# Order of masking, checks and subtractions in a fused top-k attention and feed-forward kernel

## Chip, core and metric

The kernel runs on one core of a Trainium2 chip. The metric is the device time of one execution in microseconds (us). A core has five engines that each take instructions in order from their own queue and meet through semaphores: TensorE (PE), VectorE (DVE), ScalarE (ACT), GpSimd (POOL) and SyncE (SP, which here only issues DMA transfers).

## What is computed

Batch 8, 8 heads, 576 positions, head size 64; then a feed-forward block of 4608 rows, width 512, hidden width 2048. Everything is float32.

```python
scores = scale * np.matmul(q, k.transpose(0, 1, 3, 2))
kth = np.partition(scores, -32, axis=-1)[..., -32:-31]
scores = np.where(scores >= kth, scores, -1e9)
scores = scores - np.max(scores, axis=-1, keepdims=True)
attn = np.exp(scores)
attn = attn / (np.sum(attn, axis=-1, keepdims=True) + 1e-09)
x = np.matmul(attn, v)          # then (B,H,S,D) -> (B*S, H*D)
h = x @ w_in
g = h - np.tanh(h)
out = g @ w_out
```

Of each row of 576 scores only the 32 largest keep a weight. The row's threshold is its 32nd largest score.

## The kernel before

The attention is cut into 144 steps. A step is one pair of heads and 128 query rows (or the last 64 rows of two pairs), so it holds two rows of 576 scores per partition, t = 0 and 1. The main loop in `run` runs over n and works on several steps at once, each at another stage:

- `scores(n + 1)`: PE multiplies q and k into PSUM (scps, L237), ACT copies them to SBUF (sc, L245). There is one PSUM buffer for this.
- `search(n)`: DVE finds the 32 largest of each row. It first takes the smaller and the larger of the two halves of a row (L267, L268, into one of two buffers ab), then the eight largest of the smaller halves (L270), then four rounds of the eight largest (L275) and their removal (L278). Between rounds it calls `between`, which brings in other DVE work.
- `mask(n - 1)`: POOL works out the threshold tb (L294, two small instructions) and the shift nb (L303). For t = 0 and 1 ACT writes a penalty into z (L307), zero for scores at or above the threshold, and POOL subtracts it from the score (L310). Then POOL writes the two checks `bad` (L314): whether the largest 32 of the search could have missed one among the smaller halves. The checks read ab, so the search after next, which takes the same buffer, waits for them at L267. If any check ever fails, the program runs a second time with an exact search; the profiled execution does not.
- `expo(n - 1)`: ACT takes the exponential with row sums (L330), POOL adds the epsilon (rd, L340). `invert` (DVE) and `spread` (POOL, rx, L355) prepare the division.
- Turning the weights, so that keys lie on partitions: in the 18 steps of batch 0 (`pe=True`) PE transposes z in 128 x 128 blocks (zt, L409) and ACT copies them into et (L412): two copies of 512 columns at the beginning of a step, one of 128 later. In all other steps DVE transposes 32 x 32 blocks (L376) and DMAs rearrange them (L390, on SP's queue).
- `values`: PE multiplies by v (av, L433) and turns rx (L441); ACT copies (xs, L445); POOL multiplies (xT, L457, or xTr, L448).

When all pairs of heads of a block of rows (a unit, 128 or 256 rows) are done, its feed-forward work is put on a list as small items, and `deal` spends them between the stages at a rate that a planner works out (`rate`). `ffn_h` multiplies by w_in (hps, L486); each time 512 columns are full, ACT takes tanh (th, L498) and copies h (g, L499), and POOL subtracts (g, L500). `ffn_o` multiplies g by w_out in eight parts of two blocks (ops, L507); part p reads the subtractions in the order in which they were made. ACT copies the result (ot, L517) and SP stores it. th, ot and a temporary f of the weight conversion share four buffers.

The weights are converted on the chip during steps 0 to 10 of batch 0, 32 pieces in all, two to four a step, called from `between` (`convert`): per piece DVE (L157, L163), ACT (f L158, L161, and L166), DVE (L169) and POOL (L172), before the piece's buffer takes the next load.

All of this is written out in one program order; no scheduler moves anything. In one turn of the loop the order is: `spread` and `values` of older steps; then, in batch 0, the transposes with the two large et copies; then `mask(n - 1)`; then `search(n)`; then feed-forward items, `scores(n + 1)`, the small et copy, `expo(n - 1)`, and more feed-forward items. An engine's queue has its instructions in exactly this order, so on ACT the two et copies stand ahead of the penalties, and on POOL a g subtraction of one turn stands ahead of the next turn's tb.

Of the kernel before, what the change touches and what calls it, by code (L numbers as in the profile page):

```python
# [8 lines left out]
AF = mybir.ActivationFunctionType  # L9
ALU = mybir.AluOpType  # L10
FP32 = mybir.dt.float32
# [5 lines left out]
BIG = 2.0**80  # L17
# [31 lines left out]
def kernel(  # L49
# [9 lines left out]
    nc = tc.nc  # L59
    P = nc.NUM_PARTITIONS  # L60
    B, H, S, D = q.shape
# [15 lines left out]
    scale = 1.0 / float(D) ** 0.5  # L77
# [5 lines left out]
    def pool(name, bufs, **kw):  # L83
        return ctx.enter_context(tc.tile_pool(name=name, bufs=bufs, **kw))
# [7 lines left out]
    zpool = pool("z", 2)  # L92
# [191 lines left out]
    def mask(n, exact):  # L284

        x = st[n]
        sc, m = x["sc"], x.pop("m")
        scf = sc[:].rearrange("p t s k -> p t (s k)")
        tb = mpool.tile([P, 2], FP32, tag="tb", name="tb")
        if exact:  # L290
            nc.gpsimd.tensor_scalar(tb[:], m[:, :, TOP - 1], BIG, None, ALU.mult)
        else:
            for t in range(2):
                nc.gpsimd.tensor_scalar(  # L294
                    tb[:, t : t + 1],
                    m[:, t, TOP - 1 : TOP],
                    m[:, t, TOP - 9 : TOP - 8],
                    BIG,
                    ALU.min,
                    ALU.mult,  # L300
                )
        nb = mpool.tile([P, 2], FP32, tag="nb", name="nb")
        nc.gpsimd.tensor_scalar(nb[:], m[:, :, 0], -scale, None, ALU.mult)  # L303
        z = zpool.tile([P, 2 * S], FP32, tag="z", name="z")
        zv = z[:].rearrange("p (t k) -> p t k", t=2)
        for t in range(2):
            nc.scalar.activation(  # L307
                zv[:, t, :], scf[:, t, :], AF.Relu, bias=tb[:, t : t + 1], scale=-BIG
            )
            nc.gpsimd.tensor_tensor(zv[:, t, :], scf[:, t, :], zv[:, t, :], ALU.subtract)  # L310
        if not exact:
            ab = x.pop("ab")
            for t in range(2):
                nc.gpsimd.tensor_scalar(  # L314
                    bad[:, t, n : n + 1],
                    ab[:, t, S2 + 7 : S2 + 8],
                    BIG,
                    tb[:, t : t + 1],
                    ALU.mult,
                    ALU.is_gt,  # L320
                )
        x.update(z=z, zv=zv, nb=nb)

    rds = {}
# [24 lines left out]
    def spread(n):  # L349

        if steps[n].last:
            rd = rds.pop(n)
            nq = steps[n].nq
            rx = rxs[n] = xpool.tile([P, 2, 2, D], FP32, tag="rx", name="rx")
            nc.gpsimd.tensor_copy(  # L355
                rx[:, 0:nq], rd[:, 0:nq].unsqueeze(3).to_broadcast([P, nq, 2, D])
            )
# [36 lines left out]
    def turn_pe(n):  # L394

        g, z = steps[n], st.pop(n)["z"]
        if g.rem:
            et = et_rem
        elif g.i:
            et = ets.pop(n - 1)  # L400
        else:
            et = etpool.tile([P, 4 * S], FP32, tag="et", name="et")[:]
        ets[n] = et
        et = tiles(et, g.nq)[:, :, :, g.i, :].rearrange("p a k j -> p k a j")
        for k0 in range(0, KC, J):
            kn = min(J, KC - k0)
            zt = zt_ps.tile([P, 512], FP32, tag="zt", name="zt")
            for k in range(kn):
                nc.tensor.transpose(  # L409
                    zt[:, k * P : (k + 1) * P], z[:, (k0 + k) * P : (k0 + k + 1) * P], ident[:]  # L410
                )
            nc.scalar.copy(  # L412
                et[:, k0 : k0 + kn],
                zt[:, 0 : kn * P].rearrange("p (k a j) -> p k a j", a=NG, j=G),
            )
            if k0:
                yield
# [53 lines left out]
            u.xT = p.tile([P, CD, N], FP32, tag=u.tag, name=u.tag)  # L471
        return u.xT

    cur = {}

    def ffn_h(u, item):

        w = u.n
        per = 2 * P // w
        for f in range(item * per, (item + 1) * per):  # L480
            j, fo = f // FJ, (f % FJ) * P
            s = f * w % 512
            if s == 0:
                cur[u] = h_ps.tile([P, 512], FP32, tag="h", name="hps")
            for c in range(CD):
                nc.tensor.matmul(  # L486
                    cur[u][:, s : s + w],
                    w_in[j][:, c, fo : fo + P],
                    u.xT[:, c, 0:w],
                    start=(c == 0),  # L490
                    stop=(c == CD - 1),
                )
        if item % 2:
            th = thpool.tile([P, 512], FP32, tag="th", name="th")
            if item % 4 == 1:
                u.g.append(gpool.tile([P, 2, 512], FP32, tag="g", name="g"))
            g = u.g[-1][:, item % 4 // 2, :]
            nc.scalar.activation(th[:], cur[u][:], AF.Tanh)  # L498
            nc.scalar.copy(g, cur[u][:])  # L499
            nc.gpsimd.tensor_tensor(g, g, th[:], ALU.subtract)  # L500

    def ffn_o(u, i, part):
        if part == 0:
            cur[u] = h_ps.tile([P, DM], FP32, tag="h", name="ops")
        for f in range(2 * part, 2 * part + 2):
            o = f * u.n + i * P
            nc.tensor.matmul(  # L507
                cur[u][:],
                u.g[o // 1024][:, o % 1024 // 512, o % 512 : o % 512 + P],
                w_out[f // FJ][:, f % FJ, :],  # L510
                start=(f == 0),
                stop=(f == CF - 1),
            )
        if part < CF // 2 - 1:
            return
        ot = thpool.tile([P, DM], FP32, tag="th", name="ot")
        nc.scalar.copy(ot[:], cur[u][:])  # L517
        for rows, dst in u.blocks[i]:
            nc.sync.dma_start(dst, ot[rows, :])
# [50 lines left out]
    def run(exact):  # L570
# [9 lines left out]
        for i, (b, hp) in enumerate(pairs):  # L580
            n = next(n for n, g in enumerate(steps) if (g.b, g.hp) == (b, hp))
# [56 lines left out]
        def here(i):  # L638
            return 0 <= n + i < NS

        def between(i):
            for fn in at_round.pop((n, i), []):
                fn()
            if i == 0 and here(-2):
                invert(n - 2)
                if not steps[n - 2].pe:
                    turn_z(n - 2)
# [9 lines left out]
        for u in begun:  # L657
            k = 2 if u.tag == "xT" else 1
# [5 lines left out]
        def rate():  # L664


            have, low, high = len(work), 0.0, None
            coming = sorted((t, u.n // 8) for u, t in ready.items() if t > n)
            for t, k in coming + [(NS + 4, 0)]:
                r = have / max(t - n, 1)  # L670
                high = r if high is None else min(high, r)
                have += k
            for u, t in begun.items():
                if t > n and u in before:
                    need = [i + 1 for i, x in enumerate(work) if x[1] is before[u]]
                    if need:
                        low = max(low, need[-1] / (t - n))
            return max(low, high)
# [11 lines left out]
        for n in range(-4, NS + 4):  # L690
            pe = here(-2) and steps[n - 2].pe
            if here(-3) and not steps[n - 3].pe:
                spread(n - 3)
            for m in (n - 4, n - 3):
                if 0 <= m < NS and steps[m].last and steps[m].lag == n - m:
                    values(m)
            share, usable = rate(), converted[0]
            if pe:
                w = turn_pe(n - 2)
                next(w)  # L700
            if here(-1):
                mask(n - 1, exact)
            if here(0):
                search(n, exact, between)
            elif here(-2):
                between(0)
            if here(-2) and not pe and steps[n - 2].last:
                spread_keys(n - 2)
            if pe:
                spread(n - 2)  # L710
            deal(0.4)
            if here(1):
                scores(n + 1)
            if pe:
                next(w)
            if here(-1):
                expo(n - 1)
            deal(0.2)
            if pe and steps[n - 2].last:
                values(n - 2)  # L720
            deal(0.2)
            for fn in todo.pop(n, []):
                fn()
            deal(0.2)
# [4 lines left out]
    with tc.manual_schedule():  # L729
        run(False)  # L730
# [10 lines left out]
    with tc.If(again > 0):  # L741
        with tc.manual_schedule():
            run(True)
# [29 lines left out]
```

## Time and profile before

| what | us |
|---|---|
| four runs, median | 1548.53 |
| four runs, lowest and highest | 1547.87, 1550.42 |
| the profiled execution | 1551.0 |
| its span, first to last instruction | 1549.2 |
| PE busy | 1440.7 (93%) |
| DVE busy | 1347.7 (87%) |
| POOL busy | 941.3 (61%) |
| ACT busy | 883.0 (57%) |
| chain that ended last: PE's share | 73% |
| chain that ended last: DVE's share | 10% |

Busy times are sums over the span; register, semaphore and DMA-issuing instructions are not counted. The chain that ended last is followed back from the last instruction, at each step to what released it. A line of the timeline names the start and the time of an instruction, its engine, its line in the kernel, what it writes and reads, and in brackets how long its engine had stood idle before it and which engine's work ended that. In the lists of waits a line says which engine's instruction waited for which other, and for how long in total, how many times, and the longest.

The instructions that the change moves, with the count and mean time of one:

| line | engine, what | count | mean ns |
|---|---|---|---|
| L294 | POOL, threshold tb | 288 | 299 |
| L303 | POOL, shift nb | 144 | 254 |
| L307 | ACT, penalty z | 288 | 769 |
| L310 | POOL, z subtraction | 288 | 1411 |
| L314 | POOL, check bad | 288 | 323 |
| L412 | ACT, et copy of 512 columns | 36 | 591 to 605 |
| L500 | POOL, g subtraction | 144 | 1276 |

### The profile page before, as it was taken

To read this page: it belongs to the slowest core of one execution; us is meant where nothing else is said; L and a number is where in the kernel's file an instruction comes from. 1 tells how busy PE (TensorE), PEld (TensorE's weight loads), DVE (VectorE), ACT (ScalarE), POOL (GpSimd) and SP (SyncE) were. 2 spreads that over 40 slices of the span, in tenths; PEclk is the share of its full clock that TensorE was granted. 3 is DMA by queue.
4 is the path that set the end of the run, shared out by engine and by line. 5 is a ranking of instruction groups with operands and counts; after the bars stand their busy time and mean duration, and the time that the engine had idled before them with its cause. 6 is when DMAs were issued, how large, how long until landed. Compare 5 with 4: busy or idle time off the path is not lost.

```text
span 1549.2 us, 25298 instructions
## 1 busy us (share of the span) xinstructions
PE 1440.7 (93%) x7428; PEld 912.2 (59%) x7428; DVE 1347.7 (87%) x3828; ACT 883.0 (57%) x1567; POOL 941.3 (61%) x1525
## 2 busy tenths in 40 slices
PE   2556899899999999999999999999999999999997
PEld 1345467455565665656566665656566665656673
DVE  7987889999999999999999999999999999997300
ACT  4886767556565565656565565656565565655320
POOL 3777667667565675757565675757565675746420
PEclk9777899999999999999999999999999999999999
DMA  9944113324443354234433354234443345322200
GB/s 255 359 160 159 50 28 67 89 69 94 104 92 76 83 105 103 70 78 97 103 88 79 80 107 102 70 79 97 100 90 80 80 98 110 81 64 59 73 10 16
DMA packets 258835, 147.42 MB, mean 95 GB/s; under 512 B 210048, under 2 KB 217216, under 8 KB 258688
## 3 DMA queue, kind: packets, MB, share of 16 engines
q1 hardware_dynamic: 256912, 145.49, 38.3%
q8 instruction: 62, 1.02, 0.3%
q14 instruction: 85, 0.70, 0.1%
q10 hardware_dynamic: 1776, 0.22, 0.1%
HBM read 61.85 MB, written 9.44 MB: 46 GB/s over the span
## 4 chain that ended last, share of the span: by engine, by line
PE 73%; DVE 10%; SPq 5%; ACT 4%; issue 3%; DMA 3%; POOL 2%; DVEq 0%; ACTq 0%; POOLq 0%
PE ops L507 27%; PE hps L486 26%; PE av L433 9%; PE scps L237 8%; SPq L390 4%; DVE ab L278 3%; DVE m L275 3%; PE av L441 2%; SPq L200 1%; DMA zx<-in_moe_w_in_dram 1%; ACT z L307 1%; PE zt L409 1%; DVE spare L376 1%; DVE ab L270 1%; DVE ab L267 1%
## 5 line engine op out<-in xcount | busy, mean ns | idle before, releaser
L507 PE MATMUL ops<-w_out,g 128*128 128x512 f32 x1152 | 525.4, 602 | 0.0
L486 PE MATMUL hps<-xT,w_in 128*128 128x256 f32 (+1 forms) x2176 | 473.7, 373 | 1.2 <-POOL xT L457 1.2
L275 DVE MAX8 m<-ab 128x8 f32<-128x288 f32 (+1 forms) x1152 | 464.3, 444 | 0.0
L310 POOL TENSOR_TENSOR z<-sc,z 128x576 f32<-128x576 f32 x288 | 400.2, 1411 | 83.8 <-ACT z L307 83.8
L486 PEld LDWEIGHTS hps<-xT,w_in 128*128 128x128 f32 x2176 | 392.5, 193 | 73.4 <-issue 16.0
L278 DVE MATCH_REPLACE8 ab<-m,ab 128x288 f32<-128x288 f32 x864 | 376.1, 443 | 0.0
L507 PEld LDWEIGHTS ops<-w_out,g 128*128 128x128 f32 x1152 | 212.0, 192 | 243.6 <-issue 240.0
L307 ACT ACTIVATE z<-sc,tb 128x576 f32<-128x576 f32 x288 | 207.6, 769 | 153.8 <-POOL tb L294 153.8
L500 POOL TENSOR_TENSOR g<-g,th 128x512 f32<-128x512 f32 x144 | 183.7, 1276 | 123.1 <-ACT g L499 111.1
L245 ACT COPY sc<-scps 128x1152 f32<-128x1152 f32 x144 | 160.9, 1117 | 115.9 <-PE scps L237 112.1
L330 ACT ACTIVATE z<-z,nb 128x576 f32<-128x576 f32 x288 | 221.5, 773 | 6.8 <-POOL z L310 6.6
L237 PE MATMUL scps<-kT,qT 64*128 64x288 f32 (+1 forms) x1280 | 184.5, 437 | 30.0 <-DVE qT L222 27.0
L433 PE MATMUL av<-et,vb 128*64 128x256 f32 (+1 forms) x1088 | 131.6, 377 | 46.0 <-ACT et L412 38.8
L237 PEld LDWEIGHTS scps<-kT,qT 64*128 64x128 f32 (+1 forms) x1280 | 100.0, 181 | 122.5 <-issue 59.5
L267 DVE TENSOR_TENSOR ab<-scps,sc 128x576 f32<-128x576 f32 x144 | 107.8, 749 | 71.9 <-POOL bad L314 61.2
L498 ACT ACTIVATE th<-hps 128x512 f32<-128x512 f32 x144 | 85.4, 593 | 107.9 <-PE hps L486 105.5
L457 POOL TENSOR_TENSOR xT<-xs 128x256 f32<-128x256 f32 (+1 forms) x68 | 47.2, 695 | 161.1 <-ACT xs L445 160.9
L445 ACT COPY xs<-av 128x512 f32<-128x512 f32 (+1 forms) x84 | 44.1, 525 | 164.4 <-PE av L441 164.2
L433 PEld LDWEIGHTS av<-et,vb 128*64 128x64 f32 x1088 | 74.9, 138 | 104.5 <-ACT et L412 40.8
L340 POOL TENSOR_SCALAR rd<-den 128x2 f32<-128x2 f32 x144 | 33.4, 232 | 146.7 <-ACT z L330 104.7
L270 DVE MAX8 ab<-ab 128x8 f32<-128x288 f32 x288 | 116.6, 446 | 0.0
L268 DVE TENSOR_TENSOR ab<-scps,sc 128x576 f32<-128x576 f32 x144 | 107.5, 747 | 0.0
(67 smaller groups left out, 1249.8 us busy)
## 6 DMA issues: line engine op xcount, KB each, us to landing
et<-spare SPq DMA_DIRECT2D x448, 72.0 KB, 2.0
et<-zx SPq DMA_DIRECT2D x448, 72.0 KB, 2.0
kin<-in_k_dram SPq DMA_DIRECT2D x116, 72.0 KB, 2.3
vb<-in_v_dram SPq DMA_DIRECT2D x64, 128.0 KB, 2.4
out_dram<-ot SPq DMA_DIRECT2D x32, 256.0 KB, 2.2
qin<-in_q_dram SPq DMA_DIRECT2D x113, 72.0 KB, 2.3
w_out<-in_moe_w_in_dram SPq DMA_DIRECT2D x10, 512.0 KB, 5.5
w_out<-in_moe_w_in_dram SPq DMA_DIRECT2D x10, 511.5 KB, 5.9
```

The lines of the kernel that those rows point to most:

```text
L237: nc.tensor.matmul(ps[rows, t, s, 0:S2], qT[g.b, g.hp + i][half(t), qs], kT[g.b, g.hp + i][half(t), ks], start=True, stop=True,)
L245: nc.scalar.copy(sc[:], ps[:, :, :, 0:S2])
L270: nc.vector.max(ab[:, t, S2 : S2 + 8], lo[:, t, :])
L275: nc.vector.max(m[:, t, m8], last[t] if i == rounds - 1 else cur[t])
L278: nc.vector.match_replace(nxt[t], m[:, t, m8], cur[t], NEG)
L307: nc.scalar.activation(zv[:, t, :], scf[:, t, :], AF.Relu, bias=tb[:, t : t + 1], scale=-BIG)
L310: nc.gpsimd.tensor_tensor(zv[:, t, :], scf[:, t, :], zv[:, t, :], ALU.subtract)
L330: nc.scalar.activation(x["zv"][:, t, :], x["zv"][:, t, :], AF.Exp, bias=x["nb"][:, t : t + 1], scale=scale, accum_out=den[:, t : t + 1],)
L433: nc.tensor.matmul(av[half(t), 0, cols], vb[g.b, hp][:, t, c, :] if c < J else vr[g.b, hp][:, t, :], es[:, :, (J + 1) * t + c if c < J els ...
L486: nc.tensor.matmul(cur[u][:, s : s + w], w_in[j][:, c, fo : fo + P], u.xT[:, c, 0:w], start=(c == 0), stop=(c == CD - 1),)
L500: nc.gpsimd.tensor_tensor(g, g, th[:], ALU.subtract)
L507: nc.tensor.matmul(cur[u][:], u.g[o // 1024][:, o % 1024 // 512, o % 512 : o % 512 + P], w_out[f // FJ][:, f % FJ, :], start=(f == 0), sto ...
```

## The change

Three orders change; what is computed does not.

1. In `mask` the two checks `bad` go ahead of the penalties and the z subtractions, right behind tb and nb.
2. In `run` the call of `mask(n - 1)` goes ahead of the transposes of batch 0, so that on ACT the two penalties stand ahead of the two large et copies.
3. `ffn_h` no longer issues the g subtraction. It notes the pair (g, th) in a list, and a new function `finish` issues all that are noted: behind `mask(n - 1)` of the next turn, or ahead of the first part of an output block, whichever comes first.

```diff
@@ mask
-        z = zpool.tile([P, 2 * S], FP32, tag="z", name="z")
-        zv = z[:].rearrange("p (t k) -> p t k", t=2)
-        for t in range(2):
-            nc.scalar.activation(
-                zv[:, t, :], scf[:, t, :], AF.Relu, bias=tb[:, t : t + 1], scale=-BIG
-            )
-            nc.gpsimd.tensor_tensor(zv[:, t, :], scf[:, t, :], zv[:, t, :], ALU.subtract)
         if not exact:
             ab = x.pop("ab")
             for t in range(2):
...
                     ALU.is_gt,
                 )
+        z = zpool.tile([P, 2 * S], FP32, tag="z", name="z")
+        zv = z[:].rearrange("p (t k) -> p t k", t=2)
+        for t in range(2):
+            nc.scalar.activation(
+                zv[:, t, :], scf[:, t, :], AF.Relu, bias=tb[:, t : t + 1], scale=-BIG
+            )
+            nc.gpsimd.tensor_tensor(zv[:, t, :], scf[:, t, :], zv[:, t, :], ALU.subtract)
@@
-    cur = {}
+    cur, unfinished = {}, []
+
+    def finish():
+        for g, th in unfinished:
+            nc.gpsimd.tensor_tensor(g, g, th[:], ALU.subtract)
+        unfinished.clear()
@@ ffn_h
             nc.scalar.activation(th[:], cur[u][:], AF.Tanh)
             nc.scalar.copy(g, cur[u][:])
-            nc.gpsimd.tensor_tensor(g, g, th[:], ALU.subtract)
+            unfinished.append((g, th))
@@ ffn_o
         if part == 0:
+            finish()
             cur[u] = h_ps.tile([P, DM], FP32, tag="h", name="ops")
@@ run
+            if here(-1):
+                mask(n - 1, exact)
+            finish()
             if pe:
                 w = turn_pe(n - 2)
                 next(w)
-            if here(-1):
-                mask(n - 1, exact)
```

## Prediction

> **What bounds the kernel now.** I read the page's busy shares and slices first, then busy time by stage, then the chain that ended last, then the waits of the early stage, then single steps in the timeline. The slices show two stages:
>
> ```profile
> PE   2556899899999999999999999999999999999997
> DVE  7987889999999999999999999999999999997300
> PEclk9777899999999999999999999999999999999999
> ```
>
> A slice is 38.7 us. PE fills up only after the fifth one, about 200 us in; before that neither it nor its granted clock (0.7) is full. Busy time of the engines in stretches cut at the borders of that early stage (columns: length, PE, PEld, DVE, ACT, POOL, clock, DMA share, GB/s):
>
> ```profile
> 101.00:118.00 17.00, 11.16 (x71) 9.80 (x72) 12.81 (x35) 12.11 (x22) 11.92 (x15) 0.70 0.51 189
> 118.00:133.00 15.00, 11.02 (x86) 9.65 (x85) 12.43 (x34) 11.74 (x21) 11.73 (x14) 0.84 0.39 135
> ...
> 151.00:169.00 18.00, 10.91 (x35) 4.76 (x33) 12.40 (x33) 12.41 (x22) 9.47 (x12) 0.78 0.28 104
> 169.00:213.00 44.00, 42.27 (x320) 31.12 (x321) 38.30 (x124) 31.24 (x61) 28.95 (x50) 0.93 0.10 20
> 213.00:326.00 113.00, 105.21 (x522) 62.94 (x520) 112.45 (x331) 71.98 (x132) 75.03 (x130) 1.00 0.34 74
> 326.00:1539.00 1213.00, 1206.89 (x6094) 755.50 (x6094) 1057.29 (x2999) 658.90 (x1165) 733.28 (x1203) 1.00 0.37 83
> ```
>
> From 326 us to the end PE is busy 1206.89 of 1213 us, and the chain runs over PE's lines there; from 213 to 326 DVE is busy 112.45 of 113 and the chain runs over DVE's search; from 169 to 213 PE is the fullest (42.27 of 44); from 101 to 169 nobody is full: a ring of waits. The waits of the early stage, first ACT's and POOL's from 53 to 225 us, then DVE's from 36 to 225 (total us, times, longest):
>
> ```profile
> ACT et L412 <- PE zt L409: 17.1, 16, 3.9
> ...
> ACT z L307 <- POOL tb L294: 2.8, 4, 0.7
> ```
> ```profile
> POOL g L500 <- ACT g L499: 7.2, 4, 3.1
> ```
> ```profile
> DVE f L169 <- ACT f L161: 15.7, 4, 4.9
> DVE ab L267 <- POOL bad L314: 5.4, 3, 2.8
> ```
>
> DVE waits four times, 15.7 us, for ACT's f, and ACT is late because it first sat waiting for PE's transposes (17.1 us), hardly ever for tb (2.8). POOL's own queue is held four times by a g subtraction whose input ACT has not copied yet (7.2). One such step in the timeline (start, us, engine, line, tiles, idle before and its releaser):
>
> ```profile
> 105.81 0.58 ACT L412 COPY et<-zt 128x512 f32<-128x512 f32 x1 [3.95 <-PE zt L409]
> 106.61 0.58 ACT L412 COPY et<-zt 128x512 f32<-128x512 f32 x1 [0.21 <-PE zt L409]
> 107.09 1.44 ACT L307 ACTIVATE z<-sc,tb 128x576 f32<-128x576 f32 x2
> 107.95 2.78 POOL L310 TENSOR_TENSOR z<-sc,z 128x576 f32<-128x576 f32 x2 [3.37 <-ACT z L307]
> 108.43 0.71 ACT L158 ACTIVATE f<-f,e 128x512 f32<-128x512 uint32 x1
> 109.17 0.72 ACT L161 ACTIVATE f<-f,e 128x512 int32<-128x512 f32 x1
> 109.93 1.35 DVE L169 SCALAR_TENSOR_TENSOR f<-spare,f 128x512 uint32<-128x512 uint32 x1 [3.99 <-ACT f L161]
> ```
>
> ACT idles 3.95 us, copies, and only then masks, though the threshold tb was there at 104.4. I number steps by mask: this is step 7; steps 8, 9 and 10 have their first et copy at 121.53, 138.12 and 154.97.
>
> **The change, part by part.** It removes no instruction, adds none, and issues or moves no DMA, so SP's queue is as before. PE's and DVE's orders stay; ACT's changes in the 18 steps of batch 0 alone, POOL's everywhere.
>
> *From 326 us on: 0.* The checks (2 x 0.29 us) go ahead of the two z subtractions (2.78 us a step), the g subtractions (1.28 each) behind them. Hidden by PE: it never waits for tb or bad there, and DVE, whose 61.2 us of waiting for bad look like the prize, is not the bound (1057 of 1213). A g subtraction may come some 7 us later; part p of an output block reads only the p-th subtraction of its unit, a part takes 1.72 us on PE, so the youngest has over 10 us. xT, for which PE waits 1.2 us in six small pieces, is ahead of them as before. If this cover failed, a step could lose up to one subtraction, 1.28 us.
>
> *213 to 326: 0.* DVE has no wait left to remove; the stretch starts earlier or later as a whole, and PE's 7.8 us of idle time in it let PE follow.
>
> *169 to 213: −1.5.* Three L267 wait for bad, 1.48, 2.83 and 1.10 us, the last until 213.55, where DVE's unbroken run begins. Two g subtractions sit in front of tb, at 198.34 and 207.72 (POOL had waited 1.55 and 1.83 us for ACT). With tb first and bad right behind, the next thing late is sc: PE's scps at 199.74 and 209.12, then ACT's copy (1.1 us), which ends at 202.4 and 211.8. ACT is ready a little sooner (0.3), but rx now stands behind two g subtractions: POOL would reach it at 196.07 + 0.72 + 0.56 + 0.25 + 0.57, then z from about 199.0, + 2.78 + 2.55 = 204.3 instead of 204.06, so PE's L441 slips 0.24. I let L267 start at 212.05: 213.55 − 212.05 = 1.5 gained. Bounds: 0 (PE late for another reason) to 1.8 (no slip).
>
> *Steps 7 to 10: −3.3.* Mask first puts the z pair, 1.34 us from its start to the next instruction's (107.09 to 108.43), into the idle time before et, if tb is there.
> Step 7: 3.95 idle, tb by 104.4 or sooner, since the g subtraction at 101.32 leaves: f starts at 107.1 instead of 108.43. All of 1.34 counts, and L169 meets no subtraction any more: −1.4.
> Step 8: 2.87 idle; tb, 119.81 before, comes some 0.6 sooner: ACT gains 1.2. But POOL now has a g subtraction (1.27) between z and the weight products L172, and its three L172 follow DVE's L169 one by one: z subtractions to about 124.3, DVE's group, g to 127.0, L172 at 127.0 instead of 127.48: −0.5.
> Step 9: z waits for ACT's own th and g (until 138.1), which came late from PE; ACT gains 0.75, but two g subtractions (2.55) now run from 141.7: L169 starts at 142.95, the first L172 at 145.55 instead of 144.88, the third, which frees rx and PE, at 149.5 instead of 149.02: +0.5.
> Step 10: 3.51 idle, no g pending: f 1.3 sooner, and L169 (158.78, 1.34 us) falls behind the z subtractions, which would now end at 157.2, so it takes 0.68: −1.9.
> Sum −1.4 − 0.5 + 0.5 − 1.9 = −3.3. Bounds: −5.3 (ACT's gains whole, 1.34 + 1.2 + 0.75 + 1.3, and 0.67 at L169) and, if each of the four g subtractions holds up the ring for its whole 1.27 us, +1.8 (5.1 − 3.3).
>
> *Steps 2 to 6: +0.5.* There ACT has no such gap: et at 76.73 and 77.53 with 0.54 and 0.21 idle, z at 78.01, f at 79.35. tb's first half is done at 77.0, so z would go at 77.05, end its issue at 78.39, two et copies (0.54 each) at 79.46: 0.1 later, five times. PE's ninth transpose waits for an et buffer, but stands behind scps until 79.45; the copy ends at 78.97. That is the cover; without it 0.5 a step. Bounds 0 to +2.5.
>
> *What POOL and DVE do to each other* decides the size. L169 with f and w both in SBUF took 1.28 us in the median of one group, and 0.67 where e lies in PSUM; L157 took 0.42, once 1.18, beside a z subtraction. So a meeting costs 0.67 to 0.76, and the order of steps 7 to 10 above is drawn with it. I count the meetings that I can place; steps 2 to 5 have e in PSUM and their first four DVE conversions (L157, L163 twice) still come before z's subtractions, since checks of 1.38 us a pair (126.13) fill POOL first.
>
> The Trainium skill speaks against the change here. "GPSIMD Engine Reference", section "Specifications", says that GpSimd's SBUF interfaces are shared with VectorE, with contention for DVE instructions in a two-port mode or with two SBUF inputs. By the rule alone every conversion beside any POOL instruction would suffer; by the rows, one with a PSUM input ran 0.69 us beside a z subtraction (68.55), unhurt, which the rule's second half allows for. Taking the rule at its widest, four more g subtractions would each hold DVE once, 5.1 us, and the whole gain would be gone; by the rows it is the 1.0 us or so inside the steps above.
>
> *Sum:* −1.5 − 3.3 + 0.5 = −4.3 us. The profiled execution has a span of 1549.2 and took 1551.0: 1544.9 and 1546.7. It lies 2.5 above the median of the four runs, 1548.53, to which I apply the same 4.3: **1544.2 us**. Ends: −1.8 − 5.3 + 0 = −7.1 and 0 + 1.8 + 2.5 = +4.3. One more unknown: PE's clock. Sixteen matmuls of L486 ahead of steps 7, 8 and 9 took 3.41, 2.75 and 3.62 us at the low clock, and 1.79 after 187 us; four of L507 ahead of step 10 took 3.39, and 1.72 at 181. Were the clock full there, 13.17 − 3 x 1.79 − 1.72 = 6.1 more would come. I take 0, as PE still idles there.
>
> **The rivals.**
> *Hidden anyway (1547.5).* The early ring is closed by something else: weight loads (DVE waited once, 0.7 us, for one at 165.6) or PE from 169 on. For it: PE 42.27 of 44. Against it: between 101 and 169 us PE, DVE and ACT each idle a quarter of the time or more. Then only about 1 us of the 1.5 remains.
> *Slower (1553.0): the shared memory path.* Earlier z subtractions land on DVE's conversions in steps 3 to 10, 8 x 0.76 = 6.1, and the g subtractions on L169, 4 x 0.67 = 2.7: +8.8 − 4.3 = +4.5. It takes over from the sixth extra meeting on (6 x 0.72 = 4.3), and shows as slower from the eleventh. For it: L169 at 1.28; against it: removing the wait also parts meetings, as in steps 7 and 10.
> *More (1538.1):* the clock, 4.3 + 6.1. *Not as it says:* g subtractions return to their old place where an output block starts in the same step, so POOL's head is not freed; in steps 7 to 9, which I priced, none does. That would leave the mask's move alone, within the forecast's range.
>
> **How the numbers follow.** Forecast (−3.2 to −8) 0.58, more 0.05, hidden 0.21, slower 0.16. About 0.2% (3.1 us) is what a measurement of this kernel can tell from no change. Faster 0.58 + 0.05 = 0.63, same 0.21, slower 0.16. The forecast's own range is 1540.5 to 1545.4; to leave out no more than 2 in 10 the range goes to 1539.5 below and takes in all of hidden above, to 1551.5.
>
> **What would show it.** Right: ACT's z L307 ahead of et L412 with the 3.95, 2.87 and 3.51 us waits now before et and shorter by 1.3; the three waits of L267 for bad gone before 213; DVE's unbroken run starting near 209 instead of 213.55; from 326 on PE as full as before. Wrong: L157, L163 or L169 longer in sum by over 4 us; PE waiting for g or xT after 326; the chain passing through POOL's g subtractions; or the unbroken run starting where it did.

## The result and the profile after

| | before | after |
|---|---|---|
| median, us | 1548.24 (71 runs) | 1551.04 (47 runs) |
| lowest to highest, us | 1545.09 to 1553.75 | 1547.87 to 1553.85 |
| ratio after / before, 95% interval | | 1.0018 (1.0013 to 1.0022) |
| the profiled execution, us (span) | 1551.0 (1549.2) | 1550.03 (1548.2) |

The change makes the kernel slower by 2.8 us. That is little, under the 0.2% that a few runs can tell from nothing, but with this many runs its interval lies clear of one. The two profiled executions stand the other way round, by 1.0 us: single executions of one kernel differ by several us. One piece of that can be placed: from the 35th to the 37th L267, 372 to 392 us, before lost 1.0 us on after. The clock granted to PE was 0.91 there from 360 to 380 us, and 1.00 in after; but e2 and e3 (below), without such a fall, lost 0.8 and 0.9 us on after in the same place, so the clock is not shown to be the cause. So the two profiles are compared stretch by stretch, not by their ends.

The slices of the page of after have the same two stages:

```profile
PE   2566899899999999999999999999999999999997
DVE  7998889999999999999999999999999999997300
PEclk9887899999999999999999999999999999999999
```

After 326 us PE stayed as full as it was. Busy times in the long stretch (length, PE, PEld, DVE, ACT, POOL, clock, DMA share, GB/s):

```profile
326.00:1539.00 1213.00, 1205.89 (x6096) 754.60 (x6094) 1056.73 (x3004) 659.99 (x1166) 729.48 (x1204) 1.00 0.37 83
```

PE is busy 1205.89 us, against 1206.89 before. L267's waits there (total us, times, longest), first before, then after:

```profile
DVE ab L267 <- POOL bad L314: 55.8, 59, 4.4
DVE ab L267 <- ACT sc L245: 7.2, 8, 2.8
```
```profile
DVE ab L267 <- ACT sc L245: 63.4, 55, 4.4
```

Together they are 63.0 us before and 63.4 after. The change removed the wait for bad whole, and the wait for ACT's sc grew by as much: PE, with under 8 us idle in 1213, sets the pace.

The early stage did change. Waits of ACT, of POOL and of DVE from 36 to 225 us:

```profile
ACT z L318 <- POOL tb L294: 14.1, 13, 2.5
...
ACT et L412 <- PE zt L409: 2.8, 2, 1.5
```
```profile
POOL w_out L172 <- DVE f L169: 8.7, 6, 2.6
...
POOL w_in L172 <- DVE f L169: 6.6, 4, 2.6
```
```profile
DVE ab L267 <- ACT sc L245: 5.3, 3, 2.9
```

ACT's waiting for PE's transposes is down from 18.3 us in this stretch to 2.8, but it now waits 14.1 us for tb instead of 3.2 (the prediction's 17.1 and 2.8 are from 53 us on). L267's 5.4 us for bad are gone, with 2.9 us more for sc. POOL's waiting for DVE's L169 has grown from 4.2 us, at most 1.4 at a time, to 15.3 us, up to 2.6 at a time: POOL stands between two weight products, because DVE is late with the second.

The step of the prediction's timeline (its step 7), in the timeline of after (start, us, engine, line, tiles, idle before and its releaser):

```profile
105.52 1.91 POOL L294 TENSOR_SCALAR tb<-m 128x1 f32<-128x1 f32 x2
...
105.85 0.78 ACT L318 ACTIVATE z<-sc,tb 128x576 f32<-128x576 f32 x1 [0.86 <-POOL tb L294]
...
107.45 0.78 ACT L318 ACTIVATE z<-sc,tb 128x576 f32<-128x576 f32 x1 [0.83 <-POOL tb L294]
107.47 0.57 POOL L307 TENSOR_SCALAR bad<-ab,tb 128x1 uint8<-128x1 f32 x2
...
108.00 2.78 POOL L321 TENSOR_TENSOR z<-sc,z 128x576 f32<-128x576 f32 x2
...
108.30 1.07 ACT L412 COPY et<-zt 128x512 f32<-128x512 f32 x2
...
110.73 1.27 POOL L478 TENSOR_TENSOR g<-g,th 128x512 f32<-128x512 f32 x1
110.78 1.78 DVE L169 SCALAR_TENSOR_TENSOR f<-spare,f 128x512 uint32<-128x512 uint32 x1 [1.76 <-ACT f L161]
...
112.70 1.32 POOL L172 TENSOR_TENSOR w_out<-w_out,f 128x512 f32<-128x512 f32 x1 [0.69 <-ACT f L161]
112.82 1.49 DVE L163 TENSOR_SCALAR w_out<-w_out 128x512 uint32<-128x512 uint32 x1
```

All three orders are as the diff says: checks ahead of z, masking ahead of et, the g subtraction behind z. But tb takes 1.91 us for two small instructions (0.56 in a quiet place, 1.38 in this step of before), and ACT, which now masks first, waits for each of them. L169 takes 1.78 beside the g subtraction, and L163 takes 1.49 instead of 0.41 beside the weight product.

**Steps by distance.** The steps can be measured from one L267 to the next. In the expectations and below "distance k" or "step k" is the k-th such distance; the prediction's steps, numbered by mask, are one lower (its steps 7 to 10 are distances 8 to 11, its steps 2 to 6 distances 3 to 7). The exceptions: the expectations of the first four runs, e1 to e4, still have the prediction's numbers, and so has "step 9" at 20.46 us in that of e11_defer_own, which is distance 10. Sums over groups, from the starts of L267 in each profile, and the start of the 19th L267, behind which all kernels run at DVE's pace:

| us | distances 3-7 | 8-11 | 12-16 | 19th L267 at |
|---|---|---|---|---|
| before | 63.6 | 69.3 | 45.0 | 230.0 |
| after | 67.4 | 68.5 | 44.3 | 231.5 |

The first group lost 3.8 us, the others gained 0.9 and 0.7, the first two distances another 0.8: 1.5 lost at 230 us. For all kernels below, the median time less the start of the 19th L267 in the profile is 1317.5 to 1322 us: but for some 2 us either way, what tells them apart lies before 236 us. The other 1.3 us of the 2.8 are within that scatter and are not placed.

### The profile page after: what moved, and what is told of

It reads as the page before. It is cut to its first block, busy times and chain, and to the rows that moved or that the text cites. A ratio compares the mean times of both kernels' runs of the same rounds, so it can differ in the third digit from the quotient of the medians.

```text
span 1548.2 us, 25248 instructions
## 1 busy us (share of the span) xinstructions
PE 1443.4 (93%) x7428; PEld 915.4 (59%) x7428; DVE 1352.6 (87%) x3828; ACT 882.7 (57%) x1567; POOL 934.1 (60%) x1525
## 4 chain that ended last, share of the span: by engine, by line
PE 78%; DVE 7%; SPq 6%; ACT 3%; issue 2%; POOL 2%; DMA 2%; DVEq 0%; POOLq 0%; ACTq 0%
PE ops L513 29%; PE hps L491 28%; PE av L433 9%; PE scps L237 9%; SPq L390 4%; PE av L441 2%; DVE m L275 2%; DVE ab L278 2%; SPq L200 1%; DVE f L169 1%; PE zt L409 1%; ACT et L412 1%; DMA et<-spare 1%; ACT z L318 0%; POOL w_in L172 0%
## 5 line engine op out<-in xcount | busy, mean ns | idle before, releaser
L267 DVE TENSOR_TENSOR ab<-scps,sc 128x576 f32<-128x576 f32 x144 | 107.4, 746 | 70.3 <-ACT sc L245 69.7
L445 ACT COPY xs<-av 128x512 f32<-128x512 f32 (+1 forms) x84 | 44.2, 526 | 173.9 <-PE av L441 173.6
```

## Experiments

All were timed against the kernel before on the same chip; the ratio is to that, with its 95% interval. Before itself had medians of 1547.7 to 1548.9 us beside them, so ratios are safer to compare than medians. Sums of distances are from each run's profile.

| run | what | median us | ratio | 3-7 | 8-11 | 12-16 |
|---|---|---|---|---|---|---|
| after | all three parts | 1551.04 | 1.0018 (1.0013-1.0022) | 67.4 | 68.5 | 44.3 |
| e1_checks | checks ahead alone | 1554.25 | 1.0041 (1.0025-1.0058) | 67.8 | 73.6 | 41.9 |
| e2_mask | mask ahead alone | 1544.43 | 0.9978 (0.9967-0.9990) | 63.9 | 62.7 | 44.2 |
| e3_defer | g subtractions deferred alone | 1555.19 | 1.0046 (1.0030-1.0062) | 63.6 | 72.3 | 47.4 |
| e4_no_checks | after, checks back | 1548.9 | 1.0006 (0.9995-1.0017) | 63.8 | 69.0 | 44.9 |
| e6_ahead | after, DVE's third piece earlier | 1546.64 | 0.9988 (0.9979-0.9997) | 65.6 | 66.0 | 41.6 |
| e12_mask_ahead | e2 with that order | 1545.58 | 0.9991 (0.9982-1.0000) | 64.6 | 64.8 | 43.4 |
| e13_before_own | before, own buffers for th | 1546.63 | 0.9992 (0.9983-1.0001) | 63.6 | 67.9 | 43.6 |
| e11_defer_own | e3 with own buffers | 1553.59 | 1.0030 (1.0018-1.0042) | 63.6 | 73.7 | 47.6 |
| e16_behind_rx | e11, g subtractions behind rx | 1545.54 | 0.9973 (0.9963-0.9984) | 63.6 | 68.0 | 43.3 |
| e17_mask_behind_rx | after, the same | 1546.61 | 0.9986 (0.9977-0.9995) | 67.4 | 66.5 | 41.0 |
| e14_mask_own | e2 with own buffers | 1545.35 | 0.9975 (0.9965-0.9985) | 63.8 | 65.8 | 44.9 |
| e19_late | after, parts 1 and 3 only from step 18 | 1544.58 | 0.9966 (0.9954-0.9979) | 63.8 | 64.8 | 45.5 |
| e20_twice | e1, checks also behind z | 1550.65 | 1.0005 (0.9995-1.0014) | 64.4 | 69.1 | 45.7 |
| e21_after_twice | after, the same | 1551.56 | 1.0013 (1.0004-1.0022) | 64.2 | 68.3 | 43.5 |

The first column repeats to 0.3 us between kernels with the same order there; the second scatters by some 3 us between kernels that do the same (e2, e14 and e19: 62.7, 65.8, 64.8).

### The three parts one by one

**e1_checks:** the kernel before with part 1 alone.

```diff
         nb = ...
+        (the two checks bad)
         z = ...; penalties and z subtractions
-        (the two checks bad)
```

> The kernel before with the two checks bad ahead of the z subtractions, nothing else changed. Theory A (the checks were a spacer: behind z's they kept POOL's first weight product L172 off DVE's third L163 of a step, which now takes 1.49 us instead of 0.41 in steps 3 to 9): L163 in sum 6 to 8 us longer, the early stage longer by 3 to 6 us, and the time 1.5 to 5 us above before. Theory B (masking first makes ACT wait 0.86 us for tb in each early step): L163 as before, three waits for bad gone, 0 to 1.5 us faster. Theory C (the deferred g subtractions crowd POOL): the same as B here.

**e2_mask:** part 2 alone.

```diff
+            if here(-1):
+                mask(n - 1, exact)
             if pe:
                 w = turn_pe(n - 2)
                 next(w)
-            if here(-1):
-                mask(n - 1, exact)
```

> The kernel before with mask ahead of the transposes and et copies of batch 0, nothing else changed. Theory A: L163 stays at 0.41 us, steps 7 to 10 gain as the prediction had it, 1 to 4 us faster. Theory B: f L158 of steps 3 to 6 comes 0.5 us later in the step and the whole is 1 to 3 us slower. Theory C: as A.

**e3_defer:** part 3 alone.

```diff
-            nc.gpsimd.tensor_tensor(g, g, th[:], ALU.subtract)
+            unfinished.append((g, th))
...
             if here(-1):
                 mask(n - 1, exact)
+            finish()
```

> The kernel before with the g subtractions behind the next mask, nothing else changed. Theory C: 1.5 to 4 us slower, with steps 7 to 10 and 15 to 16 longer. Theories A and B: within 1.5 us of before, since POOL has no conversions in the way before step 7.

**e4_no_checks:** the changed kernel with the checks where they were (parts 2 and 3).

```diff
-        (the two checks bad)
         z = ...; penalties and z subtractions
+        (the two checks bad)
```

> The changed kernel with the checks put back behind the z subtractions (mask first and deferred subtractions stay). Theory A: L163 back at 0.41 us, the early stage shorter than before by what the prediction had for steps 7 to 10, 2 to 5 us faster than before. Theory B or C: still 1 to 4 us slower than before.

Measured by the ratios (x 1548.2): checks +6.3 us, mask −3.4, deferral +7.1; the last two together +0.9, all three +2.8. One part is a gain and two are losses, and they do not add up: beside the other two the checks cost 1.9 us, not 6.3. Theory B falls: ACT does wait for tb when it masks first, and gains all the same. e1 and e3 each have the loss that theories A and C name, and both losses are larger than expected. e4 fits none of the theories: its time cannot be told from before, and its L163 are not back at 0.41. Their sum is 21.4 us (20.9 in after), with seven of 1.5 to 1.6 us. But only one of these lies in distances 3 to 7, and four of the seven stand beside a z subtraction, not beside L172. So the sum of L163 does not tell the kernels apart; where the meetings fall fits better.

### Why the checks cost: an instruction that kept another one away

The first group of distances tells it: 63.6 to 63.9 us wherever the checks stand behind z (e12, with its other order of conversions, 64.6), 67.4 to 67.8 where they stand ahead. An early step of before, in the timeline:

```profile
68.55 0.69 DVE L169 SCALAR_TENSOR_TENSOR f<-w_out,e 128x512 uint32<-128x512 uint32 x1
69.15 0.63 DVE L157 TENSOR_SCALAR f<-spare 128x512 uint32<-128x512 uint32 x1
...
69.48 0.98 POOL L314 TENSOR_SCALAR bad<-ab,tb 128x1 uint8<-128x1 f32 x2
...
69.70 0.41 DVE L163 TENSOR_SCALAR w_in<-spare 128x512 uint32<-128x512 uint32 x1
...
70.42 1.27 POOL L172 TENSOR_TENSOR w_in<-w_in,f 128x512 f32<-128x512 f32 x1
```

The same step of after:

```profile
69.00 0.69 DVE L169 SCALAR_TENSOR_TENSOR f<-w_out,e 128x512 uint32<-128x512 uint32 x1 [0.61 <-ACT e L161]
69.60 0.42 DVE L157 TENSOR_SCALAR f<-spare 128x512 uint32<-128x512 uint32 x1
...
69.82 1.32 POOL L172 TENSOR_TENSOR w_in<-w_in,f 128x512 f32<-128x512 f32 x1 [0.18 <-issue]
69.94 1.49 DVE L163 TENSOR_SCALAR w_in<-spare 128x512 uint32<-128x512 uint32 x1
```

The step's first weight product L172 may start as soon as DVE's first L169 is done. Before, POOL was still at the checks then, and they ran beside L157 and L163 of the third piece, cheaply for DVE (L163 took 0.41 us). With the checks gone from there, L172 starts 0.12 us ahead of L163, which ends 1.49 us after its start, 0.29 behind the end of L172 (71.14): as if L163 stood for as long as L172 runs. This happens seven times in after and in e1, once in each of the distances 4 to 10, in before not once: 7 x 1.08 = 7.6 us on DVE. Being late, DVE then gives POOL the second L169 later, so POOL's waits of 2.6 us.

Why such a delay is paid in the early distances can be read from busy times that the prediction's table leaves out (before, 36 to 101 us, which takes in distances 3 to 7):

```profile
36.00:101.00 65.00, 34.53 (x218) 25.37 (x217) 62.85 (x176) 56.41 (x101) 48.61 (x65) 0.78 0.79 286
```

DVE is busy 62.85 of 65 us and waits for another engine for 2.0 us only. The four meetings there add 4.3 us to DVE, and the group grows by 3.8 (after) and 4.2 (e1). The other three, in distances 8 to 10, are not to be told from the scatter there. The checks had no cost in their old place that shows, and worked as a spacer.

**e20_twice** and **e21_after_twice** put only the gap back: the checks stay ahead and are issued a second time behind z, so POOL does more work than in any other version.

```diff
             nc.gpsimd.tensor_tensor(zv[:, t, :], scf[:, t, :], zv[:, t, :], ALU.subtract)
+        (the two checks bad, once more)
```

> The kernel before with the checks ahead of z (which alone took 1554.3 us) and the same two checks issued once more behind the z subtractions: POOL has 2 x 0.29 us more work in each step than in either kernel. Theory A (the checks' old place kept POOL busy behind the z subtractions until DVE's third L163 was over; it is that gap which is missing): the third L163 is back at 0.41 us, L163's sum near 13.4, steps 4 to 7 together at 50 to 50.5 us instead of 54.2, the time at 1547.5 to 1549.5, as before, with more work done. Rival B (it costs because tb, nb and the checks ahead of z hold up ACT and the z subtractions): 1553 us or more, and steps 4 to 7 at 54 or longer.

> The changed kernel with the two checks issued once more behind the z subtractions. Theory A: steps 4 to 7 fall from 53.8 to 50.2 to 51 us; the deferral's cost stays, so 1547 to 1549.5 (the changed kernel with its checks only behind z took 1548.9). Rival B: 1551 or more.

The same step of e20_twice:

```profile
69.71 0.88 DVE L157 TENSOR_SCALAR f<-spare 128x512 uint32<-128x512 uint32 x1
...
70.29 0.97 POOL L324 TENSOR_SCALAR bad<-ab,tb 128x1 uint8<-128x1 f32 x2
...
70.51 0.41 DVE L163 TENSOR_SCALAR w_in<-spare 128x512 uint32<-128x512 uint32 x1
...
71.22 1.27 POOL L172 TENSOR_TENSOR w_in<-w_in,f 128x512 f32<-128x512 f32 x1
```

L163 is back at 0.41, its sum at 13.4 us as before (20.8 in e1), distances 4 to 7 at 50.75 us instead of 54.2 (a little over the band), and the time at 1.0005 of before instead of 1.0041, with intervals that do not overlap (its 1550.65 us lie above the expected band; before was at 1548.89 in these runs). So for the checks' move alone the spacer is shown: doing the checks twice is faster than doing them once in the wrong place. In the changed kernel the time does not show it: e21 took 1.0013 of before, after 1.0018. Its distances 4 to 7 fell as well, from 53.8 to 50.6, but three L163 were still hit, in distances 8 to 10, and two L157, and its distance 2 was 1.5 us longer than in after (a load came late, L163 waited 2.46 us for it instead of 1.06). At the 19th L267 its profile is 1.6 us ahead of after, but the median is not. By its distances it speaks for theory A; its time stays unexplained.

**e6_ahead** and **e12_mask_ahead** take L163 out of the way on DVE's side: the third piece's L157 and L163 come before the first piece's L169.

```diff
-            seq = [(1, k) for k in mine[:1]]
-            for k in mine[1:]:
-                seq += [(1, k), (2, k - 1)]
-            seq += [(2, k) for k in mine[-1:]]
+            seq = [(1, k) for k in mine[:2]]
+            for k in mine[2:]:
+                seq += [(1, k), (2, k - 2)]
+            seq += [(2, k) for k in mine[-2:]]
```

> The changed kernel with all its three parts; only DVE's order among the conversions is altered: L157 and L163 of a step's third piece are issued ahead of the first piece's L169, so they are over before POOL can begin the first weight product L172, which follows that L169. Theory A (checks were a spacer: without them L172 falls on the third L163, 1.49 instead of 0.41 us, seven times): L163's sum falls from 20.9 to under 15 us, steps 4 to 6 from 13.15 to 12.3 or less, and the time falls by 5 to 6 us, to 1545 to 1546. Rival A' (the collision only moves, to L169 or to the search's instructions, or ACT's late f sets the step): L163 is short again but L157, L169 or L275 grow by as much, and the time stays at 1550 to 1552.

> The kernel before with the mask ahead of the et copies alone (which took 1544.4 us) and with the conversions' order of e6_ahead. Theory A: L163's sum falls from 15.8 to about 12 us, so up to 3 to 4 us more are gained: 1540.5 to 1543. Rival A': each step's first L169, which POOL's L172 and through it the step waits for, is put off by the two instructions now ahead of it (0.75 us) wherever it was not waiting for ACT: 1544 to 1547.

e6 took 4.4 us off the changed kernel, near what theory A expected, but its reasons came out mixed. No L163 meets L172 any more, but five L157 and three L163 now take 1.5 to 2.1 us beside z or g subtractions (L163's sum 16.8 us, not under 15; L157's 21.5 instead of 15.7). Distances 4 to 6 are 12.7 to 13.1 us, not 12.3, and the first group went to 65.6 only. Why these meetings cost less than the old ones was not separated. Without an L172 in L163's way in distances 4 to 7, in e12, the order gains nothing (1545.58 against 1544.43, L163's sum unchanged at 15.8), as rival A' had it.

### Why the deferral costs: place in POOL's queue, not buffers

A step of e3 in POOL's and DVE's timeline (the prediction's step 9):

```profile
143.70 2.48 POOL L478 TENSOR_TENSOR g<-g,th 128x512 f32<-128x512 f32 x2
...
144.99 1.47 DVE L157 TENSOR_SCALAR f<-spare 128x512 uint32<-128x512 uint32 x1 [1.69 <-POOL g L478]
146.14 1.44 POOL L172 TENSOR_TENSOR w_out<-w_out,f 128x512 f32<-128x512 f32 x1
146.38 1.48 DVE L163 TENSOR_SCALAR w_out<-spare 128x512 uint32<-128x512 uint32 x1
```

L157 waits 1.69 us for a g subtraction. Its f takes turns in four buffers with th, and a deferred subtraction keeps its th. Then, with POOL at the next subtraction and at L172, L157 and L163 are hit one after the other, 1.47 and 1.48. Two theories: the buffers (D), or simply that two g subtractions stand in POOL's queue ahead of L172 and of rx (E). **e11_defer_own** gives th its own buffers; **e13_before_own** is its control.

```diff
-    thpool = pool("th", 4)
+    thpool = pool("th", 3)
...
-            rx = rxs[n] = xpool.tile([P, 2, 2, D], FP32, tag="rx", name="rx")
+            rx = rxs[n] = xrpool.tile([P, 2, 2, D], FP32, tag="rx", name="rx")
...
-            th = thpool.tile([P, 512], FP32, tag="th", name="th")
+            th = thpool.tile([P, 512], FP32, tag="tanh", name="th")
```

> The kernel before with the deferred g subtractions alone (which alone took 1555.2 us) and with th in three buffers of its own beside three for f and ot, in place of four for all; rx has one buffer instead of two to make room. Theory D (deferral costs because th and the conversions' f take turns in the same four buffers, so that DVE's L157 waits 1.4 to 1.7 us for a g subtraction that now stands behind z, and then meets L172): DVE's waits for POOL's g are gone, step 9 falls from 20.46 to 18 us or less, the time to 1549 to 1551. Rival E (it costs because the g subtractions stand in POOL's queue ahead of L172, 1.27 us each, whatever the buffers): the time stays at 1554 to 1556.

> The kernel before with the same buffers as e11_defer_own and nothing else, as its control. All theories: within 1 us of the kernel before, 1547 to 1549, since there no instruction of the early steps waits long for one of these buffers. Were the three f buffers too few, it would be slower by one conversion's turn, 2 to 5 us, and e11_defer_own would have to be read against it.

The control came to 1546.63 us, within 1.1 of before. In e11 the wait was gone and distance 10 fell from 20.46 to 17.28, as D had it, but the time stayed: 1553.59, 7.0 above the control and a little under E's band. D falls. **e16_behind_rx** then moved the g subtractions behind L172 and rx, and **e17_mask_behind_rx** did so in the changed kernel; **e14_mask_own** shows what the buffers alone do to e2. The edit of e16 against e11:

```diff
             if here(-1):
                 mask(n - 1, exact)
-            finish()
...
             if pe:
                 spread(n - 2)
+            finish()
```

> The kernel before with deferred g subtractions alone, in the buffers of e11_defer_own (which took 1553.6 us, its control without deferral 1546.6), but issued behind rx L355 and the weight products L172 of the step instead of right behind the z subtractions. Theory E (deferral costs because the g subtractions stand in POOL's queue ahead of L172 and rx; PE then waits longer for rx and in step 16 falls to the low clock, 16 matmuls in 3.6 instead of 1.95 us): the time falls to the control's, 1545.5 to 1548; steps 8 and 9 together at 31 to 32.5 us, step 16 at 9.4 to 9.7 with its 16 matmuls in 1.95. Rival F (what costs is that a g subtraction comes later than its place right behind the copy at all, because an output block or a buffer waits for it): 1551 us or more, later still than in e11_defer_own.

> The changed kernel with all its three parts in the buffers of e11_defer_own, the g subtractions behind rx and L172 as in e16_behind_rx. Theory E: the deferral's cost of 4 to 7 us is gone, the checks' stays (steps 4 to 7 at 53.8 instead of 50.1 us): 1545 to 1548. Rival F: 1551 or more.

> The kernel before with the mask ahead of the et copies alone, in the buffers of e11_defer_own. The mask ahead gains 3.4 us by itself, the buffers 1.0 (1546.6 against 1547.7, within its uncertainty). If both add: 1542.5 to 1544. If the buffers' gain was chance: 1544 to 1545.5.

e16 came to 1545.54 us, 8 under e11: E holds and F falls, here the subtractions came later at no cost, since nothing that others wait for stood behind them. (Its distances 8 and 9 were 32.8 us together, a little over what was expected, distance 16 with 8.6 under it.) Its ratio of 0.9973 even lies under that of before, as the mask ahead does; the two together, without the checks' move, were not tried. e17 took 4.4 us off the changed kernel (1.0 of it may be the buffers') with its first group still at 67.4, so the checks' loss remains in those distances. e14 lies in the band for chance: no gain of the buffers shows on top of the mask, though 1 us is not excluded.

In the distances 12 to 16 the place in the queue can have a second price. PE's timeline of after:

```profile
206.18 0.33 PE L441 MATMUL av<-ident,rx 128*128 128x128 f32 x1 [1.12 <-POOL rx L355]
206.35 3.58 PE L491 MATMUL hps<-xT,w_in 128*128 128x128 f32 x16
```

And of before:

```profile
204.41 0.34 PE L441 MATMUL av<-ident,rx 128*128 128x128 f32 x1 [0.79 <-POOL rx L355]
204.58 1.95 PE L486 MATMUL hps<-xT,w_in 128*128 128x128 f32 x16
```

PE stood 1.12 instead of 0.79 us for rx, and the next 16 matmuls took 3.58 instead of 1.95 us. In e3, e4 and e11 the pause was 1.67 to 2.64 us and these matmuls took 3.18 to 3.62; in e16, with a pause of 0.17, they took 1.95.

### Is the late part worth anything?

**e19_late:** up to step 17 only part 2; all three from step 18 on.

```diff
+        if not exact and n > 17:
+            check()
         z = ...; penalties and z subtractions
+        if not exact and n <= 17:
+            check()
...
             unfinished.append((g, th))
+            if not late[0]:
+                finish()
...
             pe = here(-2) and steps[n - 2].pe
+            late[0] = n > 18
```

> The changed kernel, but up to step 17 only the mask goes first: the checks stay behind the z subtractions and the g subtractions behind their copies there; from step 18 on all three parts are as in the change. Theory (all that the change costs is paid before 230 us; the distance from step 18's L267 to the end is 1319.8 us give or take 2 in all kernels): as with the mask ahead alone, 1543.5 to 1545.5, and the waits of L267 for bad that remain after 230 us are gone without effect. Rival (the late part is worth something, a gain that the early loss covers in the changed kernel): 1542 or less. Rival (it costs there too): 1547 or more.

As expected: 1544.58 us. The checks and the deferral are worth nothing after 230 us that these runs can tell, and no loss by them shows there. e19 and e2 beat both kernels, by 0.34% and 0.22% of before; their intervals overlap, so neither is shown to be the better one, and e2 is the smaller edit.

## Why the prediction was wrong

It gave 1544.2 us and a gain of 4.3; the change lost 2.8. The time lies within the range, on the other side of no change, and that is luck: the range's upper end was put there for a change whose gain is hidden, not for a loss. By the profiles the change loses 1.5 at 230 us, 5.8 from the forecast: 3.3 more in steps 2 to 6, 2.4 in steps 7 to 10 and 0.8 from 169 to 213, and about 0.8 less in the first two distances, for which nothing was forecast.

- **From 326 us on, 0; 213 to 326, 0: right.** The waits for bad went, sc took their place, PE was as full as before; in e19 no worth of the late part shows.
- **Steps 2 to 6, +0.5 (0 to 2.5): the step that failed.** They cost 3.8 us. The working looked at ACT's two et copies, where the delay was small as predicted (e2 and e4, with mask first and the checks behind z, have 63.9 and 63.8 against 63.6). It did not look at DVE, the full engine of this stretch. What it missed was the checks' absence. It said that checks of 1.38 us a pair "fill POOL first" and so keep z's subtractions off the first four conversions, and that came true. It never asked what follows behind the z subtractions once the checks have left: L172, which meets the third L163. Also, a meeting was priced at 0.67 to 0.76 us; this one costs 1.08. "L157, L163 or L169 longer in sum by over 4 us" was named as what would prove it wrong, and L163 alone grew by 7.5 (13.4 to 20.9); as e4 shows, the sum alone is no proof, and only four of the seven meetings lie in this group.
- **Steps 7 to 10, −3.3: mechanism of part 2 right, price of part 3 wrong.** By steps: −1.4, −0.5, +0.5, −1.9 predicted; −1.1, +0.1, +1.9, −1.8 in the profiles, −0.9 in sum. With part 2 alone the group gained 6.7, 3.5 and 4.6 us against before in the profiles of e2, e14 and e19 (e14 only 2.1 against e13, which has its buffers). The g subtractions were taken to cost one 1.27 us place in the queue in step 8 and two in step 9, less what ACT gained; alone they cost 2.9 us in the group (5.8 in e11 against its control) and 7.1 in the time. That each step hands its delay on through L172, rx and PE fits e16, but the path of it was not followed step by step. In step 9, the one furthest off, an L169, an L157 and an L163 take 1.60, 1.49 and 1.48 us beside g subtractions and L172 in after; the working had one L169 in such a place. The bounds of this step, −5.3 to +1.8, held.
- **169 to 213, −1.5: right in kind, half in size.** The distances 12 to 16 gained 0.7. The three waits for bad went and rx slipped by 0.15 against the xT ahead of it (0.24 predicted), but PE's granted clock fell to half right behind the pause, 3.58 − 1.95 = 1.6 us. The prediction had the clock only as a possible gain. DVE's unbroken run starts at 215.07 us, not near 209.
- **The rivals.** "Slower: the shared memory path" is what happened, in another place: it expected z subtractions on L157, L163 and L169 and g subtractions on L169, where the hits that decide are L172 on the third L163. In after, in the prediction's steps 3 to 10, only one L169 is lengthened by a z subtraction, three L169 and one L157 meet a g subtraction. Its price for all of them, 8.8 us, and its total of +4.5 were nearer than the forecast.

## What to carry to other kernels

Before an instruction is moved out of a queue, look at what comes up behind it, and at what that will run beside: a cheap instruction may be holding a costly one off. In a ring where every engine waits for another, place a deferred instruction behind all that others wait for, not merely behind the one that was urgent. And test the parts of a change one by one: here one part alone gains, and all three together lose.

## What was not expected of the hardware

**How a meeting is paid.** A tensor_scalar of 128x512 on DVE (L163, one input in SBUF) that starts 0.1 to 0.25 us behind a 128x512 subtraction or product on POOL takes 1.47 to 1.52 us instead of 0.41: it ends 0.3 us after POOL's. The other way round, POOL's two tiny tb instructions took 1.91 us instead of 0.56 while DVE ran four such conversions back to back (105.97 to 107.38 us in after). L169 with one input in PSUM ran 0.69 beside a z subtraction. The Trainium skill has a rule for this in "SBUF — State Buffer", section "SBUF: two separate sides": between a GpSimd instruction and a DVE instruction in a two-port mode or with two SBUF inputs, the port pair that the two engines share is locked by whichever starts first for its whole instruction, and the other stands still. These rows agree with it, if L163, which has one SBUF input, ran in a two-port mode; no view here shows the mode. The prediction leaned on the weaker wording of "contention" and on a price of 0.7 us from meetings that had started half way; the rule as stated there would have given the whole rest of POOL's instruction.

**The granted clock after short pauses.** In step 16, 16 matmuls fell to 3.2 to 3.6 us behind pauses of 1.12 (after), 1.67, 2.62 and 2.64 us, and stayed at 1.95 behind 0.17, 0.34, 0.78, 0.79 and 1.11 us. It is not the last pause alone: e21 paused 1.65 us and kept 1.95, and in e19 these matmuls took 3.22 with no such pause right ahead of them. The kept traces narrow it down. In them the granted clock keeps one value, 1.00 or 0.50, for whole multiples of 3.41 us (30.7 us, then 3.41 at 0.50 from 206.4 us in after). In the piece of 3.41 us that ends where the clock falls, PE stood idle for 1.68 us (after), 2.03 (e4), 2.27 (e11), 2.38 (e3) and 1.58 (e19). Where it did not fall, the most idle pieces of this stretch on the same grid have 1.67 us (e6), 1.60 (e21) and 1.54 (e2), and before has 1.31; after 260 us pieces of up to 1.96 us idle kept it. So these runs fit a border near half of such a piece, and where on the grid a pause falls then matters as much as how long it is. The border is not sharp here, and no run tested it.
